# Chunked attention and a routed mixture of experts on one core: the gate in four column groups, half of the wide shifts on ScalarE, later weights, other homes for gathered rows

## The chip, the core and the metric

The kernel runs on one core of a Trainium2 chip. A core has TensorE (matmuls, PE in the rows; PEld is its weight load), VectorE (DVE), ScalarE (ACT), GpSimd (POOL) and SyncE (SP, which here only issues DMAs). Matmuls write PSUM; VectorE and ScalarE copy results out of it. Time is device microseconds of one execution, from outside; the span is the time from the first to the last instruction of the profiled execution.

## What is computed

Attention in chunks of 32 queries over a window of 56 keys and 8 memory keys, then a dense expert plus one of eight routed experts per token. The reference, cut:

```python
B, H, S, D = 4, 8, 768, 64                 # chunk, left_ctx, right_ctx = 32, 16, 8; n_mem = 8
k_full = np.concatenate([mem_k, k_ctx], axis=2)
v_full = np.concatenate([mem_v, v_ctx], axis=2)
scores = scale * np.matmul(q_c, k_full.transpose(0, 1, 3, 2))
a = softmax(scores)
out[:, :, c_start:c_end] = np.matmul(a, v_full)
x = out.transpose(0, 2, 1, 3).reshape(3072, 512)
y_dense = np.maximum(x @ w1_dense, 0.0) @ w2_dense
logits = x @ w_gate                         # 512 x 8
expert_idx = np.argmax(logits, axis=1)
for e in range(8):
    h = np.maximum(x[mask] @ w1[e], 0.0)    # mask = expert_idx == e
    y_moe[mask] = gate_w[mask, None] * (h @ w2[e])
return y_dense + y_moe
```

## The kernel before

The order of the instructions on each engine is written out by hand. The 3072 tokens are 24 tiles of 128 rows, six for each of the four batches. One loop (L646) runs over the tiles and, in each iteration i, works on several tiles at different stages: `turn` (transposes the exponentials of tile i-1 on TensorE, ScalarE copies them to `aT`), `scores` (tile i: TensorE, then VectorE's maximum and subtraction), `values` and `norm` (tile i-2; 64 f32 matmuls of 64x32, then VectorE makes `xn`), `keep_x`, `turn_x` (tile i-3; POOL casts the rows, TensorE transposes `xn` into the PSUM tile `xtp`, ScalarE copies it to `x32`) and `gate` (tile i-4; four f32 matmuls, each done in two passes, with the 128x128 block of `x32` as the loaded weights and 8 columns of `wgate` streaming; all four add up in `pg`). Every third iteration `choose`, `rank` and `place` turn the logits of three tiles into places of tokens in their experts' lists; `mark` and `enter` write these into a table in PSUM (`tab`), a matmul per tile, whose left side `on` comes from POOL or VectorE.

In most iterations TensorE also does one or two steps of transposing q or k of the next batch (`transposes`, L392; `steps_at` says how many); these use the single PSUM tile `tp` and ScalarE copies it out (kbd: two copies, qT: one). The values of a window of two tiles need their v rows at a second place: `shift_v` (L364) copies 24 partitions x 1820 columns once for each half (`par`) of a window on VectorE, and two small copies on ScalarE.

Loads: POOL's queue issues q, k, weights (`next_w` in iterations `W_AT`, then one in each slot), the stores of rows to `xs`, the gathers from `xs` (`fetch`) and the scattered stores to `out`. SP's queue issues v and the memory rows. Queues run in order, so a DMA that waits holds what is issued behind it.

After tile 23 the table is finished (L746 to L761), three slots that were gathered early (`early`) and then 13 fixed and 12 looked-up slots of 128 tokens each go through `run` (L260): dense and routed first layer (32 matmuls `ph`), transposes `xt` of the next slot's rows, second layers into `xp`, `s_send`, the next gather.

## Time and profile before

| | before |
|---|---|
| three runs, us | 289.84, 293.89, 287.27 (median 289.84) |
| profiled execution, us | 289.47 |
| its span, us | 287.3 |
| mean granted TensorE clock | 0.888 |
| busy PE / PEld / DVE / ACT / POOL, us | 233.4 / 185.3 / 174.0 / 137.7 / 163.8 |
| DMA packets, MB | 51971, 37.56 |

Busy time is an average over stages with different limits, so the rows further down go stage by stage. A timeline row has a start, a length, the engine and line, the operation with what it writes and reads, a count, and in brackets the idle time of that engine just before, with what ended it; "issue" means that nothing the profile shows was waited for. The clock is a share of 2.4 GHz, so 0.5 is its lower level of 1.2 GHz.

### The profile page before, as it was taken

The page shows a single profiled execution, that of the slowest core. Times are in us where ns is not written, and L with a number is a line of the kernel's source. Part 1 is how long each engine was busy: PE and PEld are TensorE (multiplying, and loading weights), DVE is VectorE, ACT ScalarE, POOL GpSimd, SP SyncE. Part 2 cuts the span into 40 slices and gives each one's busy share as a digit, 9 for nine tenths or more (in the row PEclk, how much of TensorE's full clock was granted, in tenths as well). Part 3 has the DMA queues.
Part 4 walks back from the last instruction along what each step waited for, and adds up shares of the span by engine and source line. Part 5 has one row for each costly group of instructions (what it writes and reads, how often), then busy time and mean ns, then how long its engine had stood idle before and what let it go on. Part 6 is the DMA issues. An engine that isn't in the chain of part 4 may idle for free. (4 is left out here: it accounts for less than half of the span.)

```text
span 287.3 us, 9912 instructions
## 1 busy us (share of the span) xinstructions
PE 233.4 (81%) x4084; PEld 185.3 (64%) x4103; DVE 174.0 (61%) x433; ACT 137.7 (48%) x233; POOL 163.8 (57%) x212
## 2 busy tenths in 40 slices
PE   2546888899799998879789495899999999999910
PEld 1335777778588777768579284677777776677700
DVE  7856679876956888999650445233333567667510
ACT  3534998747664696544402033344444444444410
POOL 8940644976659384865481347777755656564320
PEclk9999999956955999985955779999999999999985
DMA  6999749899979969793589119999983323122110
GB/s 88 191 198 159 125 80 144 166 178 154 170 113 171 161 119 150 131 175 80 99 152 145 47 61 162 194 185 207 255 207 112 110 97 105 58 86 80 48 66 0
DMA packets 51971, 37.56 MB, mean 131 GB/s; under 512 B 29775, under 2 KB 48720, under 8 KB 51922
## 3 DMA queue, kind: packets, MB, share of 16 engines
q0 software_dynamic: 22976, 28.90, 53.1%
q1 hardware_dynamic: 28946, 7.98, 17.4%
q8 instruction: 34, 0.56, 0.9%
q14 instruction: 15, 0.12, 0.2%
HBM read 41.58 MB, written 10.50 MB: 181 GB/s over the span
## 5 line engine op out<-in xcount | busy, mean ns | idle before, releaser
L487 POOL CAST rows<-xn 128x512 bf16<-128x512 f32 x24 | 30.2, 1257 | 44.0 <-DVE xn L481 43.9
L216 PEld LDWEIGHTS <-wall 128*128 128x128 bf16 x704 | 44.6, 102 | 9.2 <-issue 3.6
L216 PE MATMUL ph<-xT,wall 128*128 128x128 bf16 x704 | 47.0, 227 | 2.8 <-DVE xT L208 2.5
L242 DVE SCALAR_TENSOR_TENSOR ol<-xp,gw,ol 128x512 f32<-128x512 f32 x25 | 18.8, 751 | 35.0 <-ACT ol L241 18.2
L241 ACT COPY ol<-xp 128x512 f32<-128x512 f32 x25 | 14.6, 585 | 35.5 <-PE xp L225 25.4
L500 PE MATMUL pg<-wgate,x 128*128 128x8 f32 x192 | 30.2, 284 | 1.7 <-ACT x L494 1.3
L500 PEld LDWEIGHTS pg<-wgate,x 128*128 128x128 f32 x192 | 29.1, 232 | 3.2 <-ACT x L494 3.0
L225 PE MATMUL xp<-wall,hd 128*128 128x512 bf16 x102 | 28.7, 386 | 0.7 <-issue 0.2
L470 PE MATMUL xp<-vw,aT 64*32 64x65 f32 x1536 | 25.6, 254 | 3.0 <-issue 3.0
L372 DVE COPY vw<-vw 24x1820 f32<-24x1820 f32 x24 | 26.9, 1121 | 0.7
L219 ACT ACTIVATE hd<-ph 128x512 bf16<-128x512 f32 x28 | 16.7, 597 | 21.3 <-PE ph L216 21.3
L243 POOL DMA_INDIRECT out_dram<-ol,ixt x12 | 15.0, 1252 | 20.4 <-DVE ixt L193 9.2
L414 ACT COPY kbd<-tp 64x768 bf16<-64x768 bf16 x28 | 22.2, 793 | 8.7 <-PE tp L401 8.1
L470 PEld LDWEIGHTS xp<-vw,aT 64*32 64x32 f32 x1536 | 20.0, 120 | 9.4 <-issue 7.8
L459 PE MATMUL ap<-identf,a 128*128 128x128 f32 x96 | 18.4, 324 | 5.7 <-ACT a L454 5.5
L461 ACT COPY aT<-ap 128x512 f32<-128x512 f32 x24 | 13.9, 581 | 16.3 <-PE ap L459 16.2
L219 ACT ACTIVATE he<-ph 128x512 bf16<-128x512 f32 x28 | 16.7, 597 | 10.1 <-PE ph L216 8.9
L243 POOL DMA_INDIRECT out_dram<-ol,idx x13 | 14.0, 1074 | 12.3 <-DVE ol L242 7.1
L225 PEld LDWEIGHTS <-he 128*128 128x128 bf16 x112 | 11.0, 99 | 14.5 <-ACT he L219 3.6
L492 PE MATMUL xtp<-identf,xn 128*128 128x128 f32 x96 | 19.5, 338 | 0.9 <-DVE at L570 0.9
L586 POOL TENSOR_SCALAR on<-lanes,hf,tokv 128x128 f16<-128x128 f16 x20 | 18.5, 928 | 2.4 <-PE tab L594 1.5
L401 PE MATMUL tp<-ident,kb 128*64 128x128 bf16 x192 | 10.9, 262 | 11.0 <-DMA kb<-in_k_dram 7.9
(149 smaller groups left out, 468.9 us busy)
## 6 DMA issues: line engine op xcount, KB each, us to landing
wall<-in_moe_w_dram POOLq DMA_DIRECT2D x16, 512.0 KB
vw<-in_v_dram SPq DMA_DIRECT2D x64, 64.0 KB
xs<-rows POOLq DMA_DIRECT2D x8, 385.5 KB
kb<-in_k_dram POOLq DMA_DIRECT2D x16, 192.0 KB
qb<-in_q_dram POOLq DMA_DIRECT2D x16, 192.0 KB
vw<-in_v_dram SPq DMA_DIRECT2D x32, 56.0 KB
vw<-mtpl SPq DMA_DIRECT2D x24, 65.0 KB
wall<-in_moe_w_dense_dram POOLq DMA_DIRECT2D x2, 512.0 KB
```

The lines of the kernel that those rows point to most:

```text
L216: nc.tensor.matmul(ph[:, f, :], w[:, d, 128 * f:128 * f + 128], xT[:, d, :], start=(d == 0), stop=(d == DT - 1))
L219: nc.scalar.activation(h, ph, AF.Relu)
L225: nc.tensor.matmul(xp[:, half, :], h[:, f, :], w[:, f, :], start=(f == 0), stop=(f == FT - 1))
L242: nc.vector.scalar_tensor_tensor(o, xp[:, 1, :], gw, o, op0=ALU.mult, op1=ALU.add)
L243: i = nc.gpsimd.indirect_dma_start(out[:, :], bass.IndirectOffsetOnAxis(ap=where.pop(j), axis=0), o, None, bounds_check=NTOK - 1, oob_is_e ...
L372: nc.vector.tensor_copy(dst, src)
L414: nc.scalar.copy(dst, tv[r])
L470: nc.tensor.matmul(xp[32 * cc:32 * cc + 32, par, (D + 1) * hp:(D + 1) * (hp + 1)], st["aT"][r, hp, 32 * cc:32 * cc + 32], vw[r, 4 * (g % 2 ...
L487: nc.gpsimd.tensor_copy(st["grp"]["rows"][:, st["u"], :XW].bitcast(BF16), st["xn"])
L492: nc.tensor.transpose(xtp[:, d, :], st["xn"][:, 128 * d:128 * d + 128], identf)
L500: nc.tensor.matmul(grp["pg"][:, u, :], st["x32"][:, d, :], wgate[:, d, :], start=(d == 0), stop=(d == DT - 1))
L586: eng.tensor_scalar(on, lanes, hf[:, 1, u:u + 1], tokv[:, g:g + 1], op0=ALU.is_equal, op1=ALU.mult)
```

## The change

Seven edits in one diff. (1) `wgate` is padded with zeros to 32 columns per 128-row block and becomes the loaded side: four matmuls of 32 columns, each in its own group of 32 array columns, stream the 128 tokens of `x32`; ScalarE copies the four partial results (`gparts`), and one matmul with a 0/1 matrix `pick` adds them and turns them back to tokens x 8. The first half (`gate_parts`) runs one iteration earlier, after the values, the second (`gate`) where the old one was, now behind `turn`. (2) The wide shift of the second half of each window goes to ScalarE. (3) Weights start at iteration 15, in another order, and in `run` they are issued after the gather. (4) q and k have six buffers and their loads mostly go an iteration earlier. (5) Gathered rows live in the buffers of q and k, and four fixed slots are gathered at once. (6) `rank` and the early count use the PSUM tile `tp`, and `turn_x` goes ahead of the transposing step. (7) In the last iterations two marks go earlier on POOL, the last three all to VectorE.

```diff
-QKB = 5
+QKB = 6
-W_AT = (10, 13, 16, 19, 21, 23, 24, 25, 26)
-NXG = 5
-NXE = 4
+W_AT = (15, 17, 18, 20, 21, 22, 23, 24, 25)
+AHEAD = 4
-    w_todo = [(e, half) for e in [E] + list(range(E)) for half in range(2)]
+    w_todo = [(E, 0), (0, 0), (E, 1), (0, 1)] + [(e, half) for e in range(1, E)
+                                                  for half in range(2)]
+    gates = pg.tile([128, 512], F32, name="gates")
     def fetch(j, ix, tokens=NTOK):
-        if wcs:
-            xg = wcs[0].tile([128, ROW], F32, tag="xgl", name="xgl", bufs=NXG)
-        else:
-            xg = w3.tile([128, ROW], F32, tag="xg", name="xg", bufs=NXE)
+        xg = qk_p.tile([128, ROW], F32, tag=("qb", "kb")[(len(sent) + len(where)) % 2], name="xg")
     def run(js, got, ahead=()):
         for n, j in enumerate(js):
-            next_w()
...
                 get(todo[got])
                 got += 1
+            next_w()
-        wgate = c1.tile([128, DT, E], F32, name="wgate")
+        wgate = c1.tile([128, DT, 32], F32, name="wgate")
+        pick = c1.tile([128, E], F32, name="pick")
                 dst, src = vw[r + 32:r + 56, :PC - 1], vw[r:r + 24, 1:]
-                nc.vector.tensor_copy(dst, src)
+                if par:
+                    nc.scalar.copy(dst, src)
+                else:
+                    nc.vector.tensor_copy(dst, src)
+            def gate_parts():
+                gp = gates[:, 128:256]
+                for d in range(DT):
+                    nc.tensor.matmul(gp[32 * d:32 * d + 32], wgate[:, d, :], st["x32"][:, d, :],
+                                     start=True, stop=True, tile_position=(0, 32 * d))
+                parts_t = work.tile([128, 128], F32, tag="gparts", name="gparts", bufs=1)
+                nc.scalar.copy(parts_t, gp)
+                st["parts"] = parts_t
             def gate():
                 grp, u = st["grp"], st["u"]
-                for d in range(DT):
-                    nc.tensor.matmul(grp["pg"][:, u, :], st["x32"][:, d, :], wgate[:, d, :],
-                                     start=(d == 0), stop=(d == DT - 1))
+                nc.tensor.matmul(grp["pg"][:, u, :], st["parts"], pick, start=True, stop=True)
-            rk = ps.tile([128, GRP, E], F32, tag="xtp", name="rk")
+            rk = ps.tile([128, GRP, E], F32, tag="tp", name="rk")
+        nc.gpsimd.memset(wgate, 0.0)
-        nc.sync.dma_start(wgate, moe_w_gate.rearrange("(t p) m -> p t m", p=128))
+        nc.sync.dma_start(wgate[:, :, :E], moe_w_gate.rearrange("(t p) m -> p t m", p=128))
+        nc.gpsimd.memset(pick, 0.0)
+        for d in range(DT):
+            nc.gpsimd.tensor_copy(pick[32 * d:32 * d + E], identf[32 * d:32 * d + E, 32 * d:32 * d + E])
-        qk_at = {0: 2, 1: 2, 3: 1, 5: 1, 7: 1, 8: 1, 9: 1, 11: 1, 13: 1, 14: 1}
+        qk_at = {0: 2, 1: 2, 2: 1, 4: 1, 6: 1, 7: 1, 8: 1, 10: 1, 11: 1, 13: 1}
+            do("turn", 1)
             do("gate", LAG_G)
...
-            do("turn", 1)
             do("scores", 0)
+            do("turn_x", LAG_X)
             if i > 0 and steps and steps_at[i % TPB] > 0:
                 steps.pop(0)()
-            do("turn_x", LAG_X)
             do("values", 2)
             do("norm", 2)
             do("exp", 0)
+            do("gate_parts", LAG_X)
                 mark(gm, nc.gpsimd)
+                if gm == NT - GRP - 2:
+                    mark(gm + 1, nc.gpsimd)
         for g in range(NT - GRP, NT):
-            mark(g, nc.gpsimd if g == NT - 2 else nc.vector)
+            mark(g, nc.vector)
-        for j in fixed[:NXE - NEARLY]:
+        for j in fixed[:AHEAD]:
             get(j)
-        run(early[1:], NXE - NEARLY + 2, fixed)
+        run(early[1:], AHEAD + 2, fixed)
-    ahead = NXE - NEARLY + 2
-    for j in slots[ahead:ahead + 2]:
-        get(j)
-    run(slots, ahead + 2)
+    run(slots, AHEAD + 2)
```

TensorE in an iteration without a transposing step, from `turn_x` on, before. `xtp` is the transposed x, `xp<-vw` the values, `tab` the table, `pg<-wgate` the gate, `ap` the turned exponentials, `sc` the scores:

```order
L492 MATMUL xtp<-identf,xn 128x128 x4
L470 MATMUL xp<-vw_127,aT 32x65 x32
L594 LDWEIGHTS on
L594 MATMUL tab<-cl,on 128x192
L500 MATMUL pg<-wgate,x_2721 128x8 x4
L459 MATMUL ap<-identf,a 128x128 x4
```

The same place in the change:

```order
L495 MATMUL xtp<-identf,xn 128x128 x4
L473 MATMUL xp<-vw_128,aT 32x65 x32
L503 MATMUL gates<-x_2681,wgate 32x128 x4
L604 LDWEIGHTS on
L604 MATMUL tab<-cl,on 128x192
L462 MATMUL ap<-identf,a 128x128 x4
L511 MATMUL gates<-pick,gparts 128x8
```

The gate has become two pieces, one behind the values and one behind the next iteration's `ap`.

ScalarE in iteration 3, an odd one with two transposing steps, before (`kbd` and `qT` are the copies of the steps, `x` is x32, `a` the exponentials):

```order
L461 COPY aT<-ap 128x512
L414 COPY kbd_121<-tp 64x768 x2
L494 COPY x_633<-xtp 128x512
L454 ACTIVATE a<-a 128x512
L406 COPY qT_355<-tp 128x768
```

The same iteration in the change:

```order
L464 COPY aT<-ap 128x512
L497 COPY x_630<-xtp 128x512
L417 COPY kbd_122<-tp 64x768 x2
L457 ACTIVATE a<-a 128x512
L506 COPY gparts<-gates 128x128
L373 COPY vw_129<-vw_129 24x1820
L409 COPY qT_363<-tp 128x768
```

The copy of x moved ahead of kbd, and the parts of the gate and the wide shift stand between the exponentials and qT.

POOL at the end of the attention, before, from the second but last mark on (`on` is a mark, `out_dram` the scattered store, `xs` the row store, `xg` a gather, `wall` a weight load):

```order
L487 CAST rows<-xn 128x512
L100 DMA wall<-in_moe_w_dram 128x4x512
L586 TENSOR_SCALAR on<-lanes,hf,tokv 128x128
L243 DMA out_dram<-o,idxe 3072x512
L534 DMA xs<-rows 128x3x257
L586 TENSOR_SCALAR on<-lanes,hf,tokv 128x128 x2
L184 DMA xg<-xs,idx 128x257
L100 DMA wall<-in_moe_w_dram 128x4x512
```

The same place in the change:

```order
L490 CAST rows<-xn 128x512
L596 TENSOR_SCALAR on<-lanes,hf,tokv 128x128 x2
L241 DMA out_dram<-o,idxe 3072x512
L544 DMA xs<-rows 128x3x257
L182 DMA xg<-xs,idx 128x257 x4
L241 DMA out_dram<-o,idxe 3072x512
L182 DMA xg<-xs,idx 128x257
L99 DMA wall<-in_moe_w_dram 128x4x512
```

The marks stand ahead of the scattered store, and four gathers follow each other with no store or weight load between them.

## Rows read from the trace of the kernel before

**Rows 1.** Busy by stage: length, PE, PEld, DVE, ACT, POOL; clock, DMA share, GB/s.

```profile
25.40:110.20 84.80, 76.09 (x1915) 64.35 (x1913) 64.47 (x141) 61.81 (x103) 52.45 (x66) 0.86 0.91 145
110.20:137.40 27.20, 23.78 (x615) 20.10 (x613) 24.88 (x65) 12.96 (x26) 16.07 (x18) 0.81 0.77 128
137.40:182.20 44.80, 33.60 (x379) 26.62 (x381) 19.26 (x75) 10.23 (x20) 23.07 (x28) 0.77 0.63 117
182.20:287.30 105.10, 89.55 (x1037) 66.48 (x1051) 47.01 (x108) 43.28 (x73) 56.00 (x52) 0.95 0.48 118
```

**Rows 2.** The same table for one two-step iteration and one without steps.

```profile
100.68:105.85 5.17, 4.85 (x143) 4.08 (x142) 4.72 (x14) 4.79 (x9) 4.74 (x7) 1.00 0.52 124
118.90:122.60 3.70, 3.40 (x103) 2.93 (x101) 3.50 (x7) 2.29 (x5) 2.64 (x4) 1.00 0.90 109
```

**Rows 3.** Timeline, weight loads of one tile's gate, at full and at half clock.

```profile
103.79 0.97 PEld L500 LDWEIGHTS pg<-wgate,x 128*128 128x128 f32 x8 [0.25 <-ACT x L494]
...
63.00 1.78 PEld L500 LDWEIGHTS pg<-wgate,x 128*128 128x128 f32 x8
```

**Rows 4.** Timeline, scores in four column groups at both clocks; first load of the values.

```profile
96.08 0.38 PE L438 MATMUL sc<-kbd,qT 128*32 128x112 bf16 x16
...
65.85 0.56 PE L438 MATMUL sc<-kbd,qT 128*32 128x112 bf16 x16
...
97.43 0.26 PEld L470 LDWEIGHTS xp<-vw,aT 64*32 64x32 f32 x21 [0.17 <-issue]
```

**Rows 5.** Groups by line, whole span: busy us, mean ns, idle before and its releasers.

```profile
L372 DVE COPY vw<-vw 24x1820 f32<-24x1820 f32 x24 | 26.9, 1121 | 0.7
...
L454 ACT ACTIVATE a<-a 128x512 f32<-128x512 f32 x24 | 15.1, 631 | 8.7 <-DVE a L449 8.5
L375 ACT COPY vw<-vw 24x260 f32<-24x260 f32 x16 | 6.5, 406 | 0.4
L524 ACT ACTIVATE ex<-df 128x24 f32<-128x24 f32 x8 | 1.8, 223 | 10.0 <-DVE df L514 10.0
```

**Rows 6.** An idle stretch of TensorE; a one-step iteration at half clock, as rows 1.

```profile
59.38 0.47 PE L438 MATMUL sc<-kbd,qT 128*32 128x112 bf16 x10 [0.60 <-issue]
...
84.30:90.60 6.30, 6.30 (x114) 5.41 (x113) 3.72 (x6) 2.60 (x4) 6.06 (x12) 0.50 0.96 165
```

**Rows 7.** Table by stage, 144.2 to 161.5: all work, then line 500 alone.

```profile
144.20:161.50 17.30, 16.19 (x154) 13.30 (x155) 4.70 (x19) 3.17 (x6) 6.31 (x11) 0.51 0.76 123
...
144.20:161.50 17.30, 5.50 (x24) 5.45 (x24) 0.51 0.76 123
```

**Rows 8.** Timeline of the change-over, 162 to 169 us.

```profile
162.09 0.41 DVE L208 COPY xT<-xt 128x512 bf16<-128x512 bf16 x1
...
163.28 0.32 DVE L580 CAST hf<-hl 128x6 f32<-128x6 int32 x1
...
163.73 0.32 DVE L586 TENSOR_SCALAR on<-lanes,hf,tokv 128x128 f16<-128x128 f16 x1
...
165.32 0.34 PE L594 MATMUL tab<-cl,on 128*128 128x192 f16 x1 [3.76 <-POOL on L586]
165.46 3.22 PE L216 MATMUL ph<-xT,wall 128*128 128x128 bf16 x32
...
168.74 0.41 PE L594 MATMUL tab<-cl,on 128*128 128x192 f16 x3
```

**Rows 9.** Timeline, the first gathers and the second slot's transposes.

```profile
169.91 1.22 POOL L184 DMA_INDIRECT xg<-xs,idx  x1 [3.87 <-DVE up L168]
...
174.01 1.09 POOL L184 DMA_INDIRECT xg<-xs,idx  x1 [0.31 <-issue]
...
174.97 1.95 PE L216 MATMUL ph<-xT,wall 128*128 128x128 bf16 x32
...
180.29 0.40 PE L206 MATMUL xt<-ident,xg 128*128 128x128 bf16 x4 [3.37 <-DMA xg<-xs,idx]
```

**Rows 10.** Waits, whole span: total us, times, longest.

```profile
PE tp L401 <- DMA kb<-in_k_dram: 7.9, 4, 5.0
```

More of the change, by code (lines that the diff above doesn't have):

```diff
@@ L284, in w_of @@
         return wall[:, j[0], :DT], wall[:, j[0], DT:]
+    qk_p = ctx.enter_context(tc.tile_pool(name="qk", bufs=QKB))
     with ExitStack() as one:
-        qk_p = one.enter_context(tc.tile_pool(name="qk", bufs=QKB))
         c1 = one.enter_context(tc.tile_pool(name="c1", bufs=1))
@@ L495, in turn_x @@
                 st["x32"] = x32
+            def gate_parts():
[6 more added lines that the diff above has]
+                st["parts"] = parts_t
             def gate():
                 grp, u = st["grp"], st["u"]
-                for d in range(DT):
-                    nc.tensor.matmul(grp["pg"][:, u, :], st["x32"][:, d, :], wgate[:, d, :],
-                                     start=(d == 0), stop=(d == DT - 1))
+                nc.tensor.matmul(grp["pg"][:, u, :], st["parts"], pick, start=True, stop=True)
             return {"scores": scores, "exp": expo, "turn": turn, "values": values, "norm": norm,
-                    "keep_x": keep_x, "turn_x": turn_x, "gate": gate}
+                    "keep_x": keep_x, "turn_x": turn_x, "gate_parts": gate_parts, "gate": gate}
         def wide(ap, n=GRP):
@@ L552, in rank, with counts @@
             grp["rk"] = rk
-        def counts(n):
-            cp = ps.tile([128, n], F32, tag="xtp", name="cp")
+        def counts(n, tag):
+            cp = ps.tile([128, n], F32, tag=tag, name="cp")
             for u in range(GRP):
@@ L560, in fill_early @@
         def fill_early():
-            cp = counts(HEADS)
+            cp = counts(HEADS, "tp")
             up = small.tile([128, HEADS], F32, tag="up", name="up")
@@ L675 @@
             if grp is not None and gg % GRP == 0:
-                grp["pg"] = pg.tile([128, GRP, E], F32, tag="pg", name="pg")
+                grp["pg"] = gates[:, :GRP * E].rearrange("p (u e) -> p u e", e=E)
             if i >= LAG_X and (i - LAG_X) % GRP == 0 and i - LAG_X < NT:
@@ L718 @@
             gm = gg - GRP
-            if gm >= 0 and gm // GRP != EGRP - 1:
+            if gm >= 0 and gm // GRP != EGRP - 1 and gm != NT - GRP - 1:
                 if gm % GRP == 0:
@@ L756 @@
                                        op0=ALU.add, op1=ALU.add)
-        for j in fixed[:NXE - NEARLY]:
+        for j in fixed[:AHEAD]:
             get(j)
         goals(idx[:, :NCOL], NCOL)
-        cp = counts(E)
+        cp = counts(E, "xtp")
         nc.vector.tensor_copy(cnt, cp)
```

## The prediction, made before the changed kernel was run

> **What bounds the kernel now.** I read five views: the page's slices, one table of busy time by stage, the groups by line, the timeline of single iterations, and the timeline of the change-over from attention to the experts. The profiled execution took 289.47 us, of which the span is 287.3; 2.17 us lie around it. The median of the three runs shown is 289.84, so sum and median differ by 0.4 us.
>
> The stage table [rows 1] cuts the span at the first score matmul of tiles 2 and 18, at the end of tile 23's scores, and at the second routed slot after the hand-over. I call the stretches A (25.4 to 110.2 us, tiles 2 to 17, with the transposes of the next batch in most iterations), B (110.2 to 137.4, tiles 18 to 23, no such transposes), C (137.4 to 182.2, the change-over) and D (the routed slots). TensorE is busy 76.09 of 84.8 us in A, 23.78 of 27.2 in B and 33.60 of 44.8 in C, but at a granted clock of 0.86, 0.81 and 0.77: it spends part of each at the lower of its two levels (1.2 instead of 2.4 GHz). Beside it another engine is nearly full. In A it is ScalarE in the iterations with two transpose steps: 4.79 of 5.17 us [rows 2]. In B it is VectorE: 24.88 of 27.2 us, and 3.50 of 3.70 in a single iteration at full clock [rows 1, 2]. So the question for each edit is which of the three engines it loads in which stretch.
>
> **The gate.** Before, one tile's gate is 8 weight loads of 128 f32 columns, 0.97 us in a row at full clock and 1.78 at half [rows 3], that is 0.121 and 0.223 each. The new form keeps two such loads (the adding product): 0.24 and 0.45. The padded matrix adds 8 matmuls of 32 columns that stream 128 f32 columns through four column groups. The trace has no such operation. From below: 16 bf16 matmuls in the same four groups, 112 columns each, take 0.38 us at full and 0.56 at half clock [rows 4], so 8 of them about 0.2 and 0.3. From above: nothing gained over the old 0.97 and 1.78. It is nearest to the column-group row, but f32; I take 0.30 and 0.50. The tile shape also changes once more per tile (64*32, then 128*32, then 128*128). Where the shape changes ahead of the value matmuls, their first weight load comes after 0.17 us in which nothing else is waited for [rows 4]; I charge that once per tile. New gate: about 0.71 us at full clock (saves 0.26; bounds 0 to 0.57) and 1.12 at half (saves 0.66; bounds 0 to 1.1).
>
> The Trainium skill speaks against this edit: "TensorEngine Tiling (Array Packing)", section "Key Properties", says that a change of tiling mode, not merely of tile, drains TensorE. The trace agrees at one of the four kinds of change in an iteration (the 0.17 us); at the others I see no idle time. By the page, with 0.17 us for each of 24 added drains, all on the path, 4.1 us of the saving would go; by the rows only those in stretches that TensorE bounds count.
>
> **What ScalarE gets.** Per tile one copy of 128 columns out of PSUM, and per window of two tiles one wide shift, which VectorE now does in 1.10 us [rows 5]. ScalarE has no row of that size. Its rows: 24 columns 0.223, 260 columns of the same buffers 0.406, 512 columns SBUF to SBUF 0.631 [rows 5]. The slope from 24 to 512 is 0.836 ns per column, so 1820 columns are 0.406 + 1560 x 0.836 = 1.71 us (estimate; with the slope from 24 to 260, 0.775, it is 1.61), and the 128-column copy about 0.30.
>
> **Stretch A.** ScalarE is busy 61.81 us there [rows 1]. It gains 15 gate copies (4.5) and 8 wide shifts (13.7): 80.0 us. At the share that it reaches where it is full (4.79 of 5.17, 0.927 [rows 2]) that needs 86.3 us against 84.8 now: **+1.5 us**. The TensorE time saved here buys nothing, since ScalarE is behind every step of the loop (the exponentials that the next turn needs stand behind the transposes' copies in its queue). VectorE's relief is off the path here. Bounds: 80.0 / 0.98 = 81.6 (-3.2) from below. From above: an iteration with one transpose step lasts 6.3 us at half clock, TensorE busy all through [rows 6]; with 0.66 off it is 5.6, above ScalarE's 4.6 (its sum of such an iteration), and 16 iterations at 5.6 to 6 us are 90 to 96 us (+5 to +11; I take +9). The clock falls to half where TensorE's first matmul after 58.8 us follows 0.60 us in which it waited for nothing that the profile shows [rows 6]; nothing in the change removes such gaps.
>
> **Stretch B.** VectorE loses 3 wide shifts: 24.88 - 3.3 = 21.6 us. At its present share (0.915) the stretch needs 23.6 us: **-3.6 us**. ScalarE stands at 12.96 + 6 x 0.30 + 3 x 1.71 = 19.9 us and is no bound. TensorE's 23.78 loses at least 6 x 0.26. Bounds: -4.4 (VectorE at 0.946 as in [rows 2]) and 0 (the clock at half).
>
> **Stretch C.** Three parts. (1) From 144.2 to 161.5 TensorE is busy 16.19 of 17.3 us at a clock of 0.51, 5.50 of it in 24 gate matmuls, three tiles [rows 7]. Three times 0.66, and a little for the product that no longer stands ahead of the choice: **-2.2 us** (0 to -3.3). (2) At 165.32 TensorE has stood 3.76 us, from 161.56 on, for a mark on POOL, because POOL's queue holds the scattered store and the row store ahead of its last two marks [rows 8]. The change puts both marks that remain on POOL ahead of that store and gives the last ones to VectorE. What is late next is VectorE: `hf` ends at 163.60, then three marks of two instructions each, at most 0.32 us apiece [rows 8], give about 165.4, against 168.74 for the table's last three matmuls now. But the rank now uses the transposes' PSUM tile and must wait for VectorE's xT copy, which ends at 162.50 [rows 8], when before it was done with the rest by 161.56; I give 0.5 us for it behind VectorE, and 0.5 for the 32 matmuls and four transposes ahead of the table, if they still run at half clock (3.22 us [rows 8]). The table then stands at 166.4: **-2.3 us**, and the first gather with it. (3) The next stall is 3.37 us at 180.29: the second gather, issued at 174.01 behind a store and a weight load, lands [rows 9]. Four gathers are now issued right behind each other, the second 1.22 us after the first, which goes at about 169.91 - 2.3 = 167.6. Even at the 6.3 us that it takes to land now it is there by 175.1. TensorE asks for it when the 32 matmuls of 174.97 are done, at about 174.3 (174.97 + 1.95 less 2.3 and a wait of 0.3 ahead): **-3.4 us**, at worst -2.6. Sum of C: -7.9 (bounds -5 and, with (1) at its most, -9).
>
> **At nothing.** Weights from iteration 15 and in another order: the first is used in C, ten iterations on, and each later one at least one slot ahead; if one came late, a slot would stand for its landing. The loads of q and k, one iteration earlier, with six buffers, cover the transposes; the cost without them would be waits like the four, 7.9 us in all, with which TensorE now stands for k [rows 10]. Other homes of the gathered rows change no time in D, where TensorE is busy 89.55 of 105.1 us [rows 1]. The few POOL writes for the padding stand in front of loads needed ten microseconds on.
>
> **Sum.** +1.5 - 3.6 - 7.9 = -10.0: span 277.3, and with 2.17 around it **279.5 us**.
>
> **Rivals.**
> - *The clock stays up in C.* For: the new gate streams 128 columns where the old one streamed 8, and takes less time. Against: the gap of [rows 6] is not of the gate's making. The 16.19 us at 0.51 [rows 7] would take about 10: -6, so 273; with A and B at their lower bounds too, 270.
> - *ScalarE's queue is worse than its sum.* Each wide shift stands between the exponentials and the copies that free the transposes' PSUM tile; TensorE idles more and its clock falls more often. For: the fall of [rows 6]. Against: the order of ScalarE's rows leaves TensorE work while it copies. A at +6 to +9: 284 to 288.
> - *The column groups run one behind the other*, so the gate is no cheaper. For: f32. Against: 16 matmuls in 0.38 us. A does not care; C loses 2.2 and B some of its gain: 282 to 283.
> - *Slower: the shifts on ScalarE wait for the loads of v.* On VectorE such a wait blocks little; on ScalarE the exponentials, the copies and so TensorE stand behind it. For: v is loaded only four iterations ahead. Against: all 24 shifts on VectorE had 0.7 us of idle time ahead of them in all [rows 5]. It decides from about 1.4 us on each of 11 shifts: 295.5.
>
> **How the numbers follow.** Chances: forecast (275 to 284) 0.48; clock up (269 to 275) 0.18; ScalarE's queue (284 to 289) 0.23; column groups in series 0.06; slower 0.05. Two per cent, about what a measurement of this kernel can tell from no change, is below 284.0 and above 295.6. Faster: 0.48 + 0.18 + half of 0.06 = 0.69; slower 0.05; same 0.26. The range 270 to 287 leaves out the far ends of the first and third rival and the slower case.
>
> **What would show it.** Right: in A ScalarE is busy over 90% and about 80 us; its wide shift takes 1.6 to 1.8 us; the matmuls of the gate's parts take 0.2 to 0.4 us a tile; the stalls of 3.76 and 3.37 us are gone; D is 105 us. Wrong: A far from 86 us, a new wait of TensorE for `gparts`, of ScalarE for `vw`, or a weight load that a routed slot waits for.

## The result, and the profile after

The changed kernel takes 285.84 us (median of 20 runs, 283.04 to 291.6), the kernel before 294.62 in the 20 runs beside it. Single runs of either kernel are some per cent slow, so ratios are taken over each kernel's fast runs alone, those within 1.5% of its fastest: here 0.987 (95% interval 0.982 to 0.991). The three runs from which the prediction started (289.84) lay low: over all 73 runs of the kernel before the median is 292.8. Forecast were 279.5 us, 3.6% below those three. The sign is right, but by the ratio the gain is 1.3%, and the profiled span fell by 3.2 us instead of 10.0: less than half of what was forecast. The medians of all runs put the gain higher, at 2.4 to 3.0%, since those of the kernel before spread further upward. The profiled execution took 285.93 us, its span 284.1.

First the table of busy time by stage, cut where rows 1 are cut, with the start ahead of it. Columns: stretch, length, busy us of PE, PEld, DVE, ACT and POOL, granted clock, DMA share, GB/s.

```profile
0.00:26.00 26.00, 10.38 (x146) 7.75 (x147) 17.21 (x50) 10.46 (x13) 18.42 (x58) 1.00 1.09 162
26.00:112.30 86.30, 70.81 (x1945) 55.41 (x1944) 55.04 (x128) 77.57 (x126) 44.88 (x64) 0.88 0.84 139
112.30:138.40 26.10, 20.98 (x635) 15.54 (x633) 21.14 (x60) 19.28 (x34) 14.94 (x19) 0.93 0.89 147
138.40:178.30 39.90, 30.95 (x379) 21.87 (x380) 19.14 (x77) 13.31 (x25) 20.26 (x25) 0.74 0.52 106
178.30:284.10 105.80, 90.86 (x1053) 66.40 (x1051) 47.07 (x109) 43.24 (x73) 56.25 (x53) 0.95 0.52 125
```

Against [rows 1] the start is 0.6 us longer, A 1.5 longer (forecast +1.5), B 1.1 shorter (forecast 3.6), C 4.9 shorter (forecast 7.9), D 0.7 longer (forecast 0). So 5.5 of the 6.8 us that the span misses are in B and C.

The groups by line (busy us, mean ns | idle before) price the new work:

```profile
L373 ACT COPY vw<-vw 24x1820 f32<-24x1820 f32 x12 | 20.5, 1705 | 0.3
L506 ACT COPY gparts<-gates 128x128 f32<-128x128 f32 x24 | 6.3, 263 | 6.3 <-PE gates L503 6.0
```

The wide shift takes 1.705 us on ScalarE (estimate 1.71) and hardly waits for its input (0.3 us in all); the copy of the parts takes 0.26 (0.30). The stalls of [rows 8] and [rows 9] (3.76 and 3.37 us) are gone. Three waits of TensorE are new (and `ap` waits longer in all, 10.9 against 5.5 us). The first, by the timeline, stands at the first scores of each following batch (47.8, 80.6 and 112.5 us), behind ScalarE's wide shift:

```profile
111.92 1.71 ACT L373 COPY vw<-vw 24x1820 f32<-24x1820 f32 x1
113.65 0.80 ACT L409 COPY qT<-tp 128x768 bf16<-128x768 bf16 x1
...
114.50 0.18 PE L435 MATMUL sc<-mkbd,qT 128*128 128x16 bf16 x1 [1.99 <-ACT qT L409]
```

The second stands at the end of B: VectorE's one-off work for the early slots (marks of tiles 15 to 17, lines 596 and 599) lies ahead of tile 23's maximum, so the exponentials and `ap` are late by 2.14 us. Behind it the clock is at half from 139.7 to 160.2 us, almost all of the change-over.

```profile
136.38 0.78 DVE L596 TENSOR_SCALAR on<-lanes,hf,tokv 128x128 f16<-128x128 f16 x1
137.09 0.80 DVE L599 TENSOR_SCALAR cl<-cols,hf 128x192 f16<-128x192 f16 x2
137.44 0.47 DVE L596 TENSOR_SCALAR on<-lanes,hf,tokv 128x128 f16<-128x128 f16 x1
...
138.32 0.69 DVE L450 TENSOR_REDUCE mx<-sc 128x8 f32<-128x512 f32 x1
139.12 0.69 DVE L452 TENSOR_TENSOR a<-sc,mx 128x512 f32<-128x512 f32 x1
...
139.84 0.63 ACT L457 ACTIVATE a<-a 128x512 f32<-128x512 f32 x1 [2.73 <-DVE a L452]
...
140.53 1.12 PE L462 MATMUL ap<-identf,a 128*128 128x128 f32 x4 [2.14 <-ACT a L457]
```

In the kernel before the same `ap` does not wait. The clock is at half up to 137.4 us, so TensorE's own work ahead of it lasts longer, and the old gate (`pg`) stands between:

```profile
135.56 0.69 DVE L447 TENSOR_REDUCE mx<-sc 128x8 f32<-128x512 f32 x1
...
137.08 0.63 ACT L454 ACTIVATE a<-a 128x512 f32<-128x512 f32 x1 [0.34 <-DVE a L449]
...
137.49 0.98 PE L500 MATMUL pg<-wgate,x 128*128 128x8 f32 x8
...
138.33 0.64 PE L459 MATMUL ap<-identf,a 128*128 128x128 f32 x4
```

The third is at the end of C: the rank waits for VectorE's xT, and the first gather goes 1.9 us after `idx` is ready (166.09), so that its transposes wait:

```profile
162.62 0.17 PE L551 MATMUL rk<-ecap,ones 128*128 128x24 bf16 x1 [1.57 <-DVE xT L206]
...
163.72 0.83 POOL L544 DMA_DIRECT2D xs<-rows  x1
...
165.73 0.36 DVE L772 SCALAR_TENSOR_TENSOR idx<-tab,taba 128x192 int32<-128x192 f32 x1
...
168.00 1.12 POOL L182 DMA_INDIRECT xg<-xs,idx  x1 [3.44 <-DVE gw L234]
...
170.96 0.40 PE L204 MATMUL xt<-ident,xg 128*128 128x128 bf16 x4 [1.68 <-DMA xg<-xs,idx]
```

### The profile page after: what moved, and what is told of

It reads as the page before. It is cut to its first block, busy times and chain, and to the rows that moved or that the text cites. A ratio compares the mean times of both kernels' runs of the same rounds, so it can differ in the third digit from the quotient of the medians.

```text
span 284.1 us, 10068 instructions
## 1 busy us (share of the span) xinstructions
PE 224.0 (79%) x4151; PEld 167.0 (59%) x4151; DVE 159.6 (56%) x422; ACT 163.9 (58%) x269; POOL 154.7 (54%) x217
## 5 line engine op out<-in xcount | busy, mean ns | idle before, releaser
L490 POOL CAST rows<-xn 128x512 bf16<-128x512 f32 x24 | 22.9, 953 | 55.2 <-DVE xn L484 55.1
L214 PEld LDWEIGHTS <-wall 128*128 128x128 bf16 x704 | 43.1, 100 | 9.1 <-issue 3.4
L214 PE MATMUL ph<-xT,wall 128*128 128x128 bf16 x704 | 45.7, 223 | 1.7 <-DVE xT L206 1.7
L239 ACT COPY ol<-xp 128x512 f32<-128x512 f32 x25 | 14.6, 585 | 32.3 <-PE xp L223 30.8
L223 PE MATMUL xp<-wall,hd 128*128 128x512 bf16 x112 | 29.6, 388 | 0.8 <-DVE nsl L795 0.8
L462 PE MATMUL ap<-identf,a 128*128 128x128 f32 x96 | 19.3, 336 | 12.1 <-ACT a L457 10.9
L241 POOL DMA_INDIRECT out_dram<-ol,ixt x12 | 14.9, 1241 | 22.3 <-DVE ol L240 8.6
L462 PEld LDWEIGHTS ap<-identf,a 128*128 128x128 f32 x96 | 12.6, 167 | 15.6 <-ACT a L457 12.8
L450 DVE TENSOR_REDUCE mx<-sc 128x8 f32<-128x512 f32 x24 | 16.5, 689 | 8.9 <-PE sc L441 8.6
L373 ACT COPY vw<-vw 24x1820 f32<-24x1820 f32 x12 | 20.5, 1705 | 0.3
L457 ACT ACTIVATE a<-a 128x512 f32<-128x512 f32 x24 | 15.1, 630 | 9.5 <-DVE a L452 9.1
L223 PEld LDWEIGHTS <-he 128*128 128x128 bf16 x112 | 10.7, 99 | 15.8 <-ACT he L217 4.4
L497 ACT COPY x<-xtp 128x512 f32<-128x512 f32 x24 | 14.1, 589 | 7.7 <-PE xtp L495 7.7
L596 POOL TENSOR_SCALAR on<-lanes,hf,tokv 128x128 f16<-128x128 f16 x19 | 17.1, 903 | 2.3 <-issue 1.3
```

The source lines that it names most:

```text
L214: nc.tensor.matmul(ph[:, f, :], w[:, d, 128 * f:128 * f + 128], xT[:, d, :], start=(d == 0), stop=(d == DT - 1))
L223: nc.tensor.matmul(xp[:, half, :], h[:, f, :], w[:, f, :], start=(f == 0), stop=(f == FT - 1))
L241: i = nc.gpsimd.indirect_dma_start(out[:, :], bass.IndirectOffsetOnAxis(ap=where.pop(j), axis=0), o, None, bounds_check=NTOK - 1, oob_is_e ...
L373: nc.scalar.copy(dst, src)
L462: nc.tensor.transpose(ap[:, hp, :], st["a"][:, 2 * hp:2 * hp + 2, :], identf)
L490: nc.gpsimd.tensor_copy(st["grp"]["rows"][:, st["u"], :XW].bitcast(BF16), st["xn"])
```

## The experiments

All were timed beside the kernel before, in groups of runs; the table gives their medians and the stages of one profiled execution each. The median of the kernel before lies between 290.7 and 295.4 us from group to group, so two or three us between variants of different groups say little by themselves. The stages are cut by events here: A from tile 2's first score to tile 18's, B to the end of tile 23's scores (135.0 us in the kernel before; the prediction calls the end of B in rows 1 by that name too, but it lies 2.4 us later), C to the first rectified layer of the second slot after the hand-over, D to the end. The number in brackets is the time in it at half clock (1.2 GHz), by the trace's granted clock. Two profiles of the kernel before show how far a stage differs between executions of one kernel: A by 2.3 us, B by 3.3, with the time at half clock.

| kernel | median us (runs) | A | B | C | D |
|---|---|---|---|---|---|
| before | 292.8 (73) | 84.9 (23.9) | 24.9 (7.9) | 48.3 (22.9) | 103.9 |
| before, second profile (b2) | 291.8 (4) | 82.6 (17.1) | 28.2 (18.3) | 47.8 (22.6) | 103.7 |
| changed | 285.8 (20) | 86.4 (20.5) | 23.7 (3.4) | 43.9 (20.5) | 104.4 |
| e1 shifts on VectorE | 283.1 (4) | 82.2 (6.8) | 23.1 (3.4) | 45.3 (20.5) | 104.5 |
| e2 shift behind qT | 285.8 (4) | 86.4 (17.1) | 25.9 (13.7) | 41.9 (13.7) | 104.5 |
| e3 three on VectorE | 282.1 (4) | 81.3 (3.4) | 23.9 (6.8) | 43.4 (17.1) | 105.0 |
| e8 last batch on ScalarE | 277.0 (6) | 83.5 (17.1) | 24.9 (6.8) | 40.6 (13.7) | 104.1 |
| e4 old gate | 300.7 (6) | 101.1 (58.0) | 24.5 (6.8) | 45.4 (20.5) | 105.5 |
| e11 old gate, shifts on VectorE | 296.8 (4) | 95.5 (41.0) | 28.1 (15.8) | 42.7 (28.6) | 104.0 |
| e13 parts in one group | 288.1 (4) | 88.6 (10.2) | 24.7 (3.4) | 43.0 (10.2) | 104.3 |
| e14 before + gate | 286.2 (4) | 81.9 (6.8) | 23.0 (3.4) | 47.8 (21.6) | 106.1 |
| e5 marks behind mx | 279.8 (4) | 86.8 (20.5) | 24.4 (10.2) | 35.5 (0) | 104.0 |
| e6 row store early | 282.7 (4) | 91.1 (27.3) | 25.4 (10.2) | 35.3 (3.4) | 104.0 |
| e7 rank on xtp | 283.4 (10) | 87.0 (20.5) | 24.2 (6.8) | 42.0 (17.1) | 103.7 |
| e9 = e8 + e5 + e6 | 271.9 (6) | 84.1 (13.7) | 24.9 (6.8) | 34.4 (0) | 104.3 |
| e12 = e9, weights from 18 | 271.5 (4) | 80.7 (10.2) | 25.3 (10.2) | 35.0 (6.8) | 104.2 |
| e10 = e9, new end of C | 271.2 (6) | 82.5 (10.2) | 24.6 (6.8) | 30.5 (0) | 104.5 |
| e15 = e10, marks ahead | 279.1 (4) | 82.0 (6.8) | 23.6 (3.4) | 42.4 (17.1) | 105.6 |
| e17 = e10, old loop order | 274.3 (6) | 82.1 (6.8) | 26.8 (11.9) | 34.7 (12.0) | 104.6 |
| e18 old loop order | 284.3 (6) | 91.9 (23.9) | 24.3 (3.4) | 35.8 (0) | 103.7 |

### Who should shift (e1, e2, e3, e8)

```diff
-                if par:
+                if par and False:                          # e1
+                if par and (n % 3 != 2 or b == B - 1):     # e3
+                if par and b == B - 1:                     # e8
```

e2 leaves the shift on ScalarE, but issues it behind the second transposing step in the last iteration of a batch.

> All wide shifts back on VectorE, all else as in the changed kernel (stretches of the changed kernel: A 86.3 us, tiles 2 to 17; B 26.1, tiles 18 to 23; C 39.9, change-over; D 105.8). Theory (ScalarE's queue holds A up: 77.6 us busy of 86.3, and the wide shift ahead of qT's copy stops TensorE for 2.0 us at each of three batch borders): ScalarE falls to 64 us in A, the three gaps go, A falls to 80 to 82, which is the old 84.8 less 15 gates at 0.26; B is bound by VectorE again (24.9 us of work at share 0.915) and is 26 to 27.2. Rival (A is set by TensorE and its clock, whoever shifts): A stays at 85 to 87 and clock falls are as many.

> The wide shift stays on ScalarE, but in the last iteration of a batch (three times) it is issued behind the second transposing step's qT copy instead of ahead of it. ScalarE has the same work. Theory of order (the shift's place, not its length, costs): the gaps of 1.99 us at 47.8, 80.6 and 112.5 go, A loses 4 us or more (82), B 2 us and the half-clock stretch behind its gap (23 to 24). Rival, the sum (ScalarE busy 77.6 us over 0.927 needs 84 to 86 us): the wait only moves to the next aT copy, A stays at 85 to 87.

> The wide shift of the last window of batches 0 to 2 (the three with two transposing steps in the iteration) on VectorE, the others on ScalarE. Order and sum both say faster: gaps gone, ScalarE in A 77.6 - 3.4 = 74.2, over 0.927 that is 80 us; B 23 to 24. If A stays at 85 or more, neither ScalarE's order nor its sum set A, and TensorE's clock does.

> Wide shifts on ScalarE in the last batch alone (tiles 18 to 23, where no transposing steps load it), on VectorE in the others. By the sum A is as with all shifts on VectorE (82.2 us, half clock for 6.8) and B as with those on ScalarE but without the gap at its first tile: 21.5 to 23. Total 279 to 281. If A is 85 or more again, the 82.2 was chance of the clock and not the shifts.

e2 removes the 1.99 us waits, by its timeline:

```profile
111.75 0.81 ACT L409 COPY qT<-tp 128x768 bf16<-128x768 bf16 x1
112.58 1.71 ACT L373 COPY vw<-vw 24x1820 f32<-24x1820 f32 x1
...
112.26 0.54 PE L435 MATMUL sc<-mkbd,qT 128*128 128x16 bf16 x4
```

A and the median stay where they were. So the place of the shift in the queue, the first explanation that suggested itself, isn't what costs; its time on ScalarE is. Where ScalarE has fewer or none of the shifts in A, A is 81 to 84 us in all nine profiles with the new gate (e1, e3, e8, e9, e10, e12, e14, e15, e17); where it has them all, 86 to 92 in seven (changed, e2, e5, e6, e7, e13, e18). e3 takes only three of the eight away. The longer A also has more time at half clock (10 to 27 us against 3 to 17), and these profiles don't tell what ScalarE's time costs directly from what the clock adds. The tables of e1 and e3, stretch A, and of e1, stretch B:

```profile
25.86:108.09 82.23, 66.25 (x1944) 51.79 (x1944) 64.37 (x144) 64.68 (x118) 50.43 (x63) 0.96 0.88 143
108.09:131.23 23.14, 18.72 (x558) 14.36 (x557) 21.58 (x54) 13.07 (x30) 16.35 (x18) 0.93 0.97 159
```

```profile
25.47:106.81 81.34, 65.56 (x1944) 51.47 (x1944) 58.60 (x131) 73.67 (x124) 46.81 (x63) 0.98 0.88 145
```

In B the shifts on VectorE fill it to 21.58 of 23.14 us, and B is no longer than with half of them on ScalarE (23.7). So VectorE's relief brings nothing there that the profiles show. e8's total came out below its expectation, its B (24.9) above it; its runs lie between 271 and 283 us, and its ratio to the kernel before is 0.950 (0.940 to 0.960) against the changed kernel's 0.987.

### What the gate is worth (e4, e11, e13, e14)

e4 takes the old gate into the changed kernel (no parts, four products per tile with x as weights), but at the place of the new product, behind `ap`. e11 does so with all shifts on VectorE. e14 is the kernel before with the new gate alone (`gparts` in a shared buffer, the constant `low` built later, for room). e13:

```diff
-                    nc.tensor.matmul(gp[32 * d:32 * d + 32], wgate[:, d, :], st["x32"][:, d, :],
-                                     start=True, stop=True, tile_position=(0, 32 * d))
+                    nc.tensor.matmul(gp[:32], wgate[:, d, :], st["x32"][:, d, :],
+                                     start=(d == 0), stop=(d == DT - 1), tile_position=(0, 0))
```

> The gate as before (four products per tile with x as weights, no column groups, no copy of parts), all else as in the changed kernel. By the sum of the prediction: C longer by 2.2 us (three gates at half clock), B by 1.5 (six gates at 0.26), A shorter, since ScalarE loses 3.9 us of copies: 73.7 over 0.927 is 79.5, with TensorE's 3.9 us more as the other bound. If the column groups gain nothing (in series), B and C stay at 26.1 and 39.9.

> Old gate and all wide shifts on VectorE: what is left of the change are the marks, the gathers, the weights' order and the row homes. Fourth corner of gate by shift: with both 285.8 us, gate alone 283.1, shift alone 300.7. If the two add, 298; if the shift on ScalarE hurts mainly because the old gate keeps TensorE long at half clock (A 101.1 us with 58 at half clock), A is near the 84.9 us of before and the time 286 to 290. C by the old gate's three tiles: 45 us.

> The changed kernel with the gate's eight part matmuls all in the first column group, adding up there, instead of spread over four groups (the product then takes 32 rows). If the groups run beside each other, the eight take 0.43 us spread and over 0.8 us in one group, A is ScalarE's in any case (86 to 87 us at like clock), and B and C lose 0.4 us a tile: 287 to 290. If the groups bring nothing, the eight take 0.45 us here as well and the time is that of the changed kernel, 285.8.

> The kernel before with the new gate alone (padded matrix, column groups, adding product; two small constants moved to make room): shifts on VectorE, marks, gathers and weights as before. The factors so far: gate 13.8 us without and 14.9 us with the shifts on ScalarE, the shifts 2.7 us lost with the new gate. Theory (the gate is the gain, by less time at half clock: 44 to 52 us instead of 84 to 92): 292 - 14 = 277 to 281, faster than the whole change. By the prediction's price for the gate at fixed clock (0.26 a tile where TensorE bounds, 0.66 at half clock): 285 to 289.

e13's eight part matmuls take 1.06 us at full clock, those of the changed kernel 0.43:

```profile
102.43 1.06 PE L503 MATMUL gates<-x,wgate 128*32 128x128 f32 x8
```

```profile
137.17 0.43 PE L503 MATMUL gates<-x,wgate 128*32 128x128 f32 x8
```

The groups work beside each other; the rival "in series" falls. The Trainium skill, "TensorEngine Tiling (Array Packing)", section "Key Properties", has it that different tiles work in parallel, which these two rows bear out.

The old gate costs far more than the 0.26 us a tile that the new one saves at full clock. In A of e4 TensorE is busy 88.42 of 101.13 us, at a clock of 0.71:

```profile
26.07:127.20 101.13, 88.42 (x1915) 74.37 (x1914) 55.43 (x128) 76.41 (x111) 45.21 (x65) 0.71 0.74 123
```

With the shifts on ScalarE the gate is worth 14.9 us (300.7 to 285.8), without them 13.7 (296.8 to 283.1), most of it in A and by the clock: 58 against 20.5 and 41 against 6.8 us at half clock. Alone on the kernel before it is worth 6.6 (292.8 to 286.2): the theory (277 to 281) was wrong here, and the prediction's price at fixed clock (285 to 289) held. The gate alone is as fast as the whole change. Its C gains nothing, since the product now waits 2.23 us for `gparts` behind the same marks of VectorE, and the old stall for POOL's mark stays (4.04 us at 158.87):

```profile
135.63 0.39 PE L506 MATMUL gates<-pick,gparts 128*128 128x8 f32 x2 [2.23 <-ACT gparts L501]
```

Old gate and old shifts in the changed kernel (e11) are slower than the kernel before by 2.5% (ratio 1.025, 1.013 to 1.037), with A at half clock for 41 us against 17 to 24. What in the rest of the change does that was not found. `ap` waits 10.3 us in e11, against 5.5 and 4.8 in the two profiles of the kernel before, where the gate stands ahead of it; that order was tested with the new gate alone (e17 and e18 below), so with the old one it stays a candidate.

### The change-over (e5, e15, e6, e7)

e5 moves VectorE's block of the early slots behind tile 23's `mx` and `a`; e15 undoes that in the fastest version:

```diff
             do("scores", 0)
+            if gg == GRP * EGRP + 1:
+                fill_early()
+                mark(gg - 4, nc.vector)
+                mark(gg - 3, nc.gpsimd)
+                mark(gg - 2, nc.vector)
...
-            if gg == GRP * EGRP:
-                fill_early()
-                mark(gg - 3, nc.vector)
-                mark(gg - 2, nc.gpsimd)
-                mark(gg - 1, nc.vector)
```

> VectorE's fill and marks for tiles 15 to 17 (2.3 us in a row, 135.9 to 138.1) are issued behind mx and a of tile 23 instead of ahead of them, all else as in the changed kernel. Then ap of tile 23 no longer stands 2.14 us for its exponentials. Theory (the clock falls behind a gap: the fall at 139.7 comes 1.3 us behind the start of this one): the 20.5 us at half clock in C shrink to 7 us or less and C (43.9 us, counted from tile 23's last score to the second routed slot) loses 5 to 8. Rival (the work there pulls the clock down whatever stands ahead of it; before, the clock fell at 144.2 with no gap over 0.9 us for 18 us): half clock stays at 17 to 20 us, C loses 2.1 at most, or nothing if the marks are then waited for.

> The fastest version (C 30.5 us, none of it at half clock) with the fill and marks back ahead of mx and a of tile 23, so that ap of tile 23 again stands 2.1 us. Theory (the gap brings the half clock of C): half clock in C is back, 10 to 20 us of it, and C is 30.5 + 2.1 + 0.31 times that, 36 to 39. Rival (C at full clock was chance, or comes from the other edits): C is 32.6 us, at full clock.

Stretch C in e5, then in e15, and the wait that e15 brings back:

```profile
137.59:173.13 35.54, 26.77 (x479) 19.75 (x482) 21.92 (x88) 14.92 (x28) 23.44 (x29) 1.00 0.69 132
```

```profile
131.52:173.95 42.43, 34.30 (x482) 23.82 (x482) 19.52 (x78) 14.39 (x28) 23.36 (x29) 0.80 0.61 120
```

```profile
135.75 0.66 PE L462 MATMUL ap<-identf,a 128*128 128x128 f32 x4 [2.13 <-ACT a L457]
```

C is 8.4 us shorter in e5 (43.9 to 35.5) and 11.9 longer in e15 (30.5 to 42.4): 2.1 us of each are the wait, the rest goes with 20.5 and 17.1 us at half clock. e15's C lies above its expectation of 36 to 39. The medians move by 6.0 (285.8 to 279.8) and 7.9 us (271.2 to 279.1); with each set against the kernel before in its own group, it is 3.3 and 4.4. The two profiles show more than the other runs do: over all runs, by their mean clock, the time at half clock goes from 52 to 40 us in e5 and from 29 to 35 in e15. At 0.31 us for each (see b2 below), with the 2.1 us of the wait, that is an estimated 5.9 and 4.1 us.

The tie of gap and clock isn't strict. In the nine variants of the changed kernel with a wait of 1.9 us or more at tile 23's `ap` (changed, e1, e2, e3, e6, e7, e8, e15) or at the product ahead of it (e18), C is at half clock for 14 us on average, but for 3.4 in e6 and 0 in e18; in the five without such a wait (e5, e9, e10, e12, e17) for 4, but 12 in e17. With the old gate the half clock is there with the wait or without: e4 waits 2.14 us like the changed kernel and has 20.5 us of it, e11 doesn't wait and has 28.6, the kernel before 22.9 and 22.6. The row of e4:

```profile
155.78 0.66 PE L462 MATMUL ap<-identf,a 128*128 128x128 f32 x4 [2.14 <-ACT a L457]
```

e6 moves `weigh` and the last row store up to right behind the choice; e7 gives the rank its old PSUM tile back:

```diff
-            rk = ps.tile([128, GRP, E], F32, tag="tp", name="rk")
+            rk = ps.tile([128, GRP, E], F32, tag="xtp", name="rk")
```

> The last group's weights and its row store are issued right behind the choice instead of behind the rank, so POOL stores the rows ahead of the early slot's scatter; all else as in the changed kernel. Theory: the first four gathers wait for the landing of that store (issued 163.72; idx is ready at 166.1, the first gather goes at 168.0), so the gather goes at 166.1 and TensorE's wait of 1.67 us for xg is gone: C 43.9 to 42.2. Rival: the gather waits for something else (the scatter ahead, POOL's own queue) and C stays.

> The rank's PSUM tile is the one of turned x again (as before the change), not that of the transposes; all else as in the changed kernel. The wait of 1.57 us for VectorE's xT copy ahead of the rank goes. Theory: VectorE's copies of o and xT end at 162.56 in any case and the places and marks follow them, so the table's last three products come at most 0.35 us earlier, and C gains 0.3 to 0.5 us; rival (the wait is fully on the path): C loses 1.57.

```profile
160.71 0.84 POOL L544 DMA_DIRECT2D xs<-rows  x1 [1.86 <-issue]
162.42 1.09 POOL L241 DMA_INDIRECT out_dram<-o,idxe  x1 [0.88 <-DVE o L240]
166.15 1.16 POOL L182 DMA_INDIRECT xg<-xs,idx  x1 [2.64 <-DVE idx L774]
...
169.19 0.40 PE L204 MATMUL xt<-ident,xg 128*128 128x128 bf16 x4
```

In e6 the gather goes when `idx` is ready and TensorE no longer waits for it: it had waited for the row store's landing. (Its short C is mostly that little of it ran at half clock.) In e9, where the store's landing is late in spite of its early issue, the trace names it:

```profile
158.02 1.10 POOL L182 DMA_INDIRECT xg<-xs,idx  x1 [4.34 <-DMA xs<-rows]
```

In e7 the rank's wait is gone and the next user of xT has it, 1.15 of the 1.57 us:

```profile
160.07 0.18 PE L551 MATMUL rk<-ecap,ones 128*128 128x24 bf16 x1
...
161.80 1.95 PE L214 MATMUL ph<-xT,wall 128*128 128x128 bf16 x32 [1.15 <-DVE xT L206]
```

### Together (e9, e10, e12)

e10 has, besides e9's three edits, early slot 2's xT ahead of early slot 1's `o` on VectorE, the rank ahead of `o`, and the table in two halves, one slot apart:

```diff
-        run(early[1:], AHEAD + 2, fixed)
-        table()
+        run(early[1:], AHEAD + 2, fixed)
+        half_table = table()
+        run(fixed[:1], AHEAD + 2, fixed[1:])
+        table_rest(*half_table)
```

> Three edits of the earlier runs together: wide shifts on ScalarE in the last batch alone, fill and marks behind mx and a of tile 23, the last row store ahead of the early slot's scatter. If their gains are those of their stretches and add up: A 82 to 84 us, B 23 to 25, C 35.5 less 1.7 = 33.8 with no half clock, D 104: span 270 to 273, 272 to 275 us. If C's 35.5 us without half clock was chance of the clock, C is 38 to 42 and the time 277 to 280.

> As the run with the three edits, and the end of C in another order: xT of the second early slot ahead of the first one's o on VectorE, the rank on the PSUM tile of turned x and ahead of o, and the second half of the slot table one slot later. Theory: TensorE's 1.57 us ahead of the rank falls to 0.3 or less, since xT starts when its transposes end; the 1.49 us that a routed slot's matmuls wait for xT behind the table (3.4 us of VectorE in a row) go; the table's last products may wait up to 0.9 us. C 1.5 to 2.5 us less than with the three edits alone. Rival: the waits only move behind the table or to the gathers: 0 to 0.5 us.

> The three edits, and the expert weights loaded from iteration 18 instead of 15, eight instead of nine before the hand-over. With the shifts back on VectorE the value matmuls of tile 13 or 14 waited 2.4 and 2.9 us for v (97.3 and 97.4 us); the first three weight loads (iterations 15, 17 and 18) share the DMA engines with the last loads of v, k and q. Theory: these waits go and A loses 2 to 3 us more than with the three edits alone, at the price of a weight load that a routed slot may wait for. Rival: the loads of v of iterations 10 to 12 are late for other reasons (q and k in the same engines), as the waits come before the weights do: no change in A.

e9's gains add up as expected. e10's C is 3.9 us shorter than e9's, at full clock in both:

```profile
132.92:163.42 30.50, 26.37 (x478) 19.61 (x482) 18.98 (x79) 14.38 (x27) 21.69 (x27) 1.00 0.68 141
```

The medians, 271.9 and 271.2, don't tell the two apart. e10 is 6.4% faster than the kernel before (ratio 0.936, 0.922 to 0.950) and 14.6 us by medians faster than the changed one. e12 shows no wait for v in A, but one of 2.6 us ahead of the values in B (120.1 us, see the last section), and the same time: the later weights bring nothing that can be measured.

### The loop's order on TensorE (e18, e17)

```diff
-            do("turn", 1)
             do("gate", LAG_G)
...
+            do("turn", 1)
             do("scores", 0)
-            do("turn_x", LAG_X)
             if i > 0 and steps and steps_at[i % TPB] > 0:
                 steps.pop(0)()
+            do("turn_x", LAG_X)
```

> The changed kernel with TensorE's order in the loop as before the change: the gate's product ahead of the turning of a (ap), and the transposing step ahead of the turning of x. The prediction gave this move no price. In the changed kernel ap waits 10.9 us in 8 waits for its exponentials, in the kernel before 4.8 to 5.5, with the gate alone in the old order 4.8. Theory (the product ahead of ap covers part of the wait for the exponentials; the gaps there bring half clock): waits of ap fall to 5 to 8 us, A by 2 to 4, time 281 to 284. Rival (ScalarE's queue sets A with the shifts in it, the wait only moves to the product or to x): A stays 85 to 87 and the time at 285 to 287.

> The fastest version so far (271.2 us, A 82.5, waits of ap for exponentials 10.4 us) with that same old order of the loop. Theory: waits of ap fall to 5 to 6 us, A to 79 to 81 and B by 0.5, time 267 to 270. Rival: another wait of the ring from scores to values takes its place (A 82 to 84, time 270 to 273).

The theory fell: neither A got shorter (91.9 and 82.1 us). e18's waits, whole span (total, times, longest):

```profile
PE gates L503 <- ACT x L497: 9.0, 12, 1.3
...
PE gates L511 <- ACT gparts L506: 5.6, 10, 2.3
PE ap L462 <- ACT a L457: 4.8, 2, 2.6
```

In the changed kernel `ap` waits 10.9 us and the parts for x 1.6. The wait only moves along the ring from scores over exponentials to values and x.

### The kernel before again (b2)

> The kernel before, unchanged, for a second profile of it. Its 31 further runs have a median of 292 us or so against the 289.84 of the three that the prediction started from, and over them the span follows the time at half clock (71 to 113 us) at about 0.35 us for each us. If the difference of its runs is the clock alone, a profile at 292 us or more has D at 104, and the excess in A, B and C goes with more time at half clock there.

The profiled execution is only a little longer than the first one (span 288.7 against 287.3), so it can't show the kernel at 292 us and more; but it has 18.3 us at half clock in B where the first had 7.9, and B is 3.3 us longer. Over 53 runs of the kernel before for which the mean clock is known, half-clock time (worked out from that clock and the span) is 79 us on average (57 to 118) and correlates with the span at 0.88, 0.31 us of span for each us; over 20 of the changed kernel it is 52 (45 to 68), 0.86 and 0.34. So most of the difference between the two kernels goes with 27 us less at half clock (8 to 9 us), and some 3 us of other cost stand against it.

## Why the prediction missed

- **Gate price: the sum right, in part by luck.** The parts take 0.43 us and the product 0.29 at full clock, 0.72 against an estimated 0.71; at half clock 0.65 and 0.44 to 0.59, 1.09 to 1.24 against 1.12. But the parts were put at 0.30 (the prediction's own mark for being right was 0.2 to 0.4), the product at 0.24, and 0.17 us were charged for one more change of tile shape, which isn't in the 0.72. The prediction saw idle time at one kind of change only; the kernel before has 0.18 us at a second, ahead of the table's weight load at 131.20.
- **ScalarE's new work: right.** 1.705 and 0.26 us against 1.71 and 0.30.
- **A, "+1.5": right in size, and the sum's reason holds in part.** ScalarE is busy 77.57 of 86.3 us (forecast 80.0 of 86.3, so 0.90 instead of 0.927), and A is long where it has all the shifts: with fewer or none A is 81 to 84. That the length agrees to 0.1 us is luck: A of the kernel before differs by 2.3 between two executions. Wrong is "the TensorE time saved here buys nothing": with the old gate beside the same shifts A is 101.1 us. The step set one engine as the bound and left out that TensorE's load and clock are the other.
- **B, "-3.6": failed.** The step divided VectorE's remaining work by its old share of 0.915, as if VectorE were the bound. In this cut it would be 21.3 us; no profile with the new gate has less than 23.0, and with VectorE's work undiminished B is 23.1 (e1) and 23.0 (e14). The tiles run in a ring over three engines; relief of one that is 91% busy did not shorten it. What B gained is no more than the gate alone gives (e14).
- **C, "-7.9": two terms near, one missing.** (1) Gates at half clock: 1.5 us (45.4 to 43.9, e4 and the changed kernel, both 20.5 us at half) against 2.2. (2) and (3): both old stalls are gone, and the table's last three matmuls stand at 165.04 (forecast 166.4). The 0.5 us for the rank was 1.57, but it hides VectorE's own lateness (e7). The gathers were given no wait for the row store; they had one, so the first went at 168.00 (forecast 167.6), and TensorE stood 1.68 us behind it (e6). The missing term is the largest: the prediction has no wait at tile 23's `ap`. There TensorE now comes to VectorE's 2.3 us block before that is done, because it runs at full clock where the kernel before ran at half, and because `ap` stands ahead of the gate and no longer behind it. The cheaper gate isn't needed for it: e4, with the old gate in the new order, waits the same 2.14 us. Nor is the order: with the new gate in the old order (e14, e18) the product waits 2.2 us instead. The wait and the half clock behind it are worth 6.0 us by medians (e5) and 7.9 (e15), or 3.3 and 4.4 against their own groups.
- **"At nothing": not contradicted** for the weights (e12), nor for the loop's order with the new gate (e17, e18), to which the prediction gave no price. D is 0.7 us longer, the start 0.6; not followed up.
- **Rivals.** "The clock stays up in C" (273) did not happen: C had 20.5 us at half clock against 22.9. It was put aside with the argument that the gap of [rows 6] isn't of the gate's making; the gap that counted was another one. With it removed C of the profiled execution ran at full clock, at 279.8 us. "ScalarE's queue is worse than its sum": the time fell into its stretch (284 to 288), but not for its reason: A came out at the sum's +1.5, and the order didn't matter (e2). "In series" fell (e13). ScalarE's shifts did not wait for v.
- **Left open.** Why the old gate with the rest of the change (e11) holds TensorE at half clock longer than the kernel before did, why the old gate needs no such gap for half clock in C, and why the half clock behind a like gap lasts 3 us in one kernel and 20 in another.

## What to carry to other kernels

Time saved on the engine that bounds a stretch surfaces at its next meeting with another engine: look for one-off blocks (here 2.3 us of marks) that stand ahead of the loop's own work on that engine, and move them behind it. An engine that is 91% busy in a ring of dependent steps isn't thereby its bound: divide by its share only where nothing else comes back as a wait. And where TensorE changes clock, price a gap by what it does to the clock behind it, and judge stages by length and time at half clock together, over several executions.

## What the hardware showed unexpectedly

The three forms of the gate differ more in the time at half clock than in their own length: on average over runs 92 us of half clock with the old one (e4, 6 runs, 300.7 us), 52 with four column groups (285.8) and 32 with all parts in one group (e13, 288.1), although in e13 TensorE has more to do.

Between equal rank matmuls (line 553) TensorE stood 2.5 to 3.0 us in e8, e9 and e10, with the DMA engines full (share 1.03 to 1.08 in B), and e12 and e17 have 2.6 and 2.3 us of the same kind ahead of values. In e9's waits:

```profile
PE rk L553 <- issue: 3.0, 1, 3.0
```

The views name no wait here, but the trace has the packets of DMA queue 8, which the page lists as `instruction` (34 of them, 0.56 MB). In e9 such a load of 16 KB ran from 125.56 to 126.55 us, and TensorE, idle since 125.39, went on at 128.41. Over all 20 profiles 63 idle stretches of TensorE of 0.45 us or more (from 20 us on) are put to "issue", and 58 of them end 1.1 to 1.9 us behind the end of such a load, where about 12% of all moments between 26 and 180 us lie so. The 0.60 us of [rows 6] is one of them (load from 56.80 to 57.74, first matmul at 59.38). So TensorE most likely stood for its own instructions; no run tested it.
